# Early loads into the places of late weights, deeper places for exponents, POOL in the normalising, weights decoded in one width

## The chip, the cores and the metric

The kernel runs on one core of one Trainium2 chip. The metric is the device time of one execution in microseconds. One profiled execution, on which the rows below are read, took 704.23 us.

## The reference

Attention with four sink positions and a window of 128, over 4 batches, 8 heads, 768 positions and 64 columns a head, in float32; then a two-layer network on 3072 tokens of 512 columns, with 2048 hidden columns. Everything is checked at float32 accuracy; the weights arrive as float64.

```python
scores = scale * np.matmul(q, k.transpose(0, 1, 3, 2))
keep = is_sink | in_window
scores = np.where(keep, scores, -1000000000.0)
a = np.exp(scores - np.max(scores, axis=-1, keepdims=True))
a = a / (np.sum(a, axis=-1, keepdims=True) + 1e-09)
attn = np.matmul(a, v).astype(np.float32)
x = attn.transpose(0, 2, 1, 3).reshape(B * S, H * D)
h = x @ w_in
g = h - np.tanh(h)
out = (g @ w_out).astype(np.float32)
```

## The kernel before

**Tiling.** The 3072 tokens are 12 chunks of 256 (`chunks`, 3 in a batch). The first three chunks are the first chunks of batches 0 to 2. The attention of a chunk is four units, one for each pair of heads; unit `u` is pair `u % 4` of chunk `u // 4`. The network has 8 weight groups (`NG`), each with 256 hidden columns: `w_in` of a group is `(0, g)` and `w_out` is `(1, g)`. One step of the network is one chunk with one group, so there are 96 steps: 24 matmuls of the first half (L661, output `h`) and 12 of the second half (L709, output `o`). A product in float32 accuracy is made of a high part and a low part: `xh`, `xl`, `gh`, `gl`, and for weights two halves of a tile `w`.

**One unit.** `load_qk` loads keys and queries. `scores` multiplies them for two blocks of 128 queries, t = 0 and t = 1 (L457, or L450 for the first 12 units, which are called raw and use float32 as it is). `merge` (DVE: L468 and two of L474) applies the masks and takes the largest score; `exponent` (ACT, L482) exponentiates. `normalise` sums on DVE (L502, L503), scales on ACT (four of L508), and copies the sink columns on POOL (`sinks`, L513 to L515, tile `z`). `turn` transposes on PE (L532, tile `t`) and copies into the place `pts[:, m]`: once on ACT (`whole`, L539) and twice on DVE with masks (`part`, L546, below and after). `attend` closes a pair of units in the first three chunks: a transpose of `z` on PE (L563), copies of it on ACT (`zr`, L570), the product with the sink values (L580) and 16 matmuls with the values (L586), then `xh` on ACT (L598) and `xl` on DVE (L602). I call the 16 of L586 "the values".

**Weights.** `load_w` loads a group in two halves, `z` = 0 and 1, into tiles that are later overwritten by the decoded weights. `weights` turns each half of 512 numbers from float64 words into float32 with three operations on DVE (`_decode_part`, L154, L156, L158, tile `wm`), makes the high part on ACT (L634) and the low part on DVE (L640). All 16 tiles `(k, g)` have places of their own and stay to the end.

**Places.** Exponents `p` have two places (pool `pp`), chosen by `u % 2`. The copies of the transposes have four (`m = u % 4`). Raw queries have two tiles, so that the load of unit u waits for unit u - 2. Zeros around the queries of raw units are written by POOL for units 2 and 3 alone (L103), since later ones write on the same spots.

**Order.** The order of instructions on each engine is planned by `Work.order`: each piece of work has an engine, an assumed duration, a due time, and what it reads and writes. The planner runs through them and takes, on an engine that is free, the ready piece that is due first. `WAKE` is the assumed time from one engine's end to another's start, and `SLACK` comes on top where the waiting engine is PE. Engines then work strictly in that order, SP (which issues the loads) too. Steps of the network are ordered as `order` says: groups 0 and 1 for the first three chunks, then groups 2 to 7 for chunks 2 and 1, then chunk 0, then chunk after chunk.

**Ends.** The sums of the second half are kept in PSUM: `bank` says where (one tile `o` with two halves for most chunks). `collect` copies a half on ACT (L719) and `store` writes it out.

Of the kernel before, what the change touches and what calls it, by code (L numbers as in the profile page):

```python
# [9 lines left out]
F32 = mybir.dt.float32  # L10
# [156 lines left out]
class Work:  # L167
# [4 lines left out]
    WAKE = 80  # L172
    SLACK = 250
# [17 lines left out]
    def order(self):  # L191
# [15 lines left out]
        while any(waiting.values()):  # L207
# [9 lines left out]
            for u in users[n]:  # L217
                f = self.all[u][0]
                lag = 0 if f == e else self.WAKE + (self.SLACK if f == "PE" else 0)
# [7 lines left out]
def _banded(tc, qd, kp, vp, vs, masks, w_in, w_out, ident, pts, early, out):  # L227
    nc = tc.nc
    et = mybir.EngineType
    with ExitStack() as ctx:  # L230
# [6 lines left out]
        pp, sm = pool("pp", 2), pool("sm", 2)  # L237
# [6 lines left out]
        RAW, TWO, CUT, SPLIT, DUO = 12, 12, 2, 0, 3  # L244
# [8 lines left out]
        FIRST, EARLY, PACE, LEAD = 55000.0, 5000.0, 7200.0, 16000.0  # L253
        UNIT, SECOND, WLEAD, WNEXT = 3400.0, 0.0, 9000.0, 3500.0
# [22 lines left out]

        def unit(u):
            cc, p = divmod(u, NPAIR)
            return (cc, p, *chunks[cc])  # L280

        def slots(u):
            return [("kt", u if u < 2 else u % 2 + 2), ("qt", u if u < 2 else u % 2 + 2)]

        def load_qk(u):
            cc, p, b, c = unit(u)

            def keys():
# [12 lines left out]
            t = due_unit(u) - 8000
            work.add("SP", 500, t, keys, (), [slots(u)[0], "seq k"], lands=800)
# [27 lines left out]
        def load_w(k, g):  # L330
            def words():
                for z in range(2):
                    t = wraw[k, g, z] = wpool.tile([P, WG], I32, tag=f"w{k}_{g}_{z}", name=f"wraw{k}_{g}_{z}")
                    nc.sync.dma_start(t, (w_in, w_out)[k][g].bitcast(I32)[:, z * WG : (z + 1) * WG])

            t = due_group(g) + 3000 * k - 24000
            work.add("SP", 1000, t, words, (), [("wr", k, g)], lands=4100)
# [100 lines left out]
        def scores(u, t):  # L438
# [55 lines left out]
            work.add("DVE", 880 if kind else 450, d + 1000, merge, s + ["mask"] * (0 < kind), [("p", u % 2, i) for i in range(t, 2)])  # L494
            work.add("ACT", 780, d + 2000, exponent, (), [("p", u % 2, t)])

        def normalise(u):
# [11 lines left out]

            def sinks():  # L510
# [7 lines left out]
            ps = [("p", u % 2, 0), ("p", u % 2, 1)]  # L518
# [493 lines left out]
```

## Time and profile before

| | |
|---|---|
| median of three runs | 704.1 us (703.26 to 705.12) |
| the profiled execution | 704.23 us |
| its span in the trace | 702.5 us |
| PE busy in the span | 683.6 us (97%) |
| DVE busy | 437.4 us (62%) |
| ACT busy | 371.4 us (53%) |
| POOL busy | 49.3 us (7%) |

A busy PE is not a PE at its peak: its matmuls are pipelined and their ends are modelled. The page divides the span into slices and gives for each the busy share of an engine and the clock that PE was granted, as a share of the full one. The windows give the same for stretches that one chooses. Idle time is put down to the engine and the line that ended it, in square brackets in the timeline, behind a bar in the groups.

### The profile page before, as it was taken

What the parts mean: (1) busy time and instruction counts of PE and PEld (TensorE: products, weight loads), DVE (VectorE), ACT (ScalarE), POOL (GpSimd) and SP (SyncE); (2) the same over time, 40 slices, a digit from 0 to 9 for tenths busy, and PEclk for the clock granted to TensorE, in tenths of its full rate; (3) what the DMA queues carried; (4) which work ended last, traced back from release to release, by engine and by line L of the source; (5) the groups of instructions that cost most, each with busy time, mean ns of one, the idle gap of its engine ahead of it and who ended that gap; (6) DMA issues with size and microseconds to landing.
All of it is one profiled execution on the core that took longest, in us unless ns stands there. A gap on an engine that the chain in (4) does not pass through costs nothing.

```text
span 702.5 us, 12478 instructions
## 1 busy us (share of the span) xinstructions
PE 683.6 (97%) x4604; PEld 603.1 (86%) x4604; DVE 437.4 (62%) x1148; ACT 371.4 (53%) x1017; POOL 49.3 (7%) x186
## 2 busy tenths in 40 slices
PE   6979999999999999999999999999999999999996
PEld 4657889999989989988988998898898988998985
DVE  6898999984866456645665664664654755664121
ACT  5977443345756456545655555465555645644222
POOL 3221010000100000000001000001000000000000
PEclk9989999999999999999999999999999999999999
DMA  5877900002212012112103112111112101100001
GB/s 177 285 254 277 389 9 1 5 25 72 72 57 84 27 50 85 53 27 87 53 28 106 28 54 76 39 46 70 53 28 87 54 27 54 60 1 2 31 1 35
DMA packets 31713, 52.14 MB, mean 74 GB/s; under 512 B 3228, under 2 KB 21020, under 8 KB 31644
## 3 DMA queue, kind: packets, MB, share of 16 engines
q1 hardware_dynamic: 31644, 51.26, 22.5%
q8 instruction: 38, 0.62, 0.4%
q14 instruction: 31, 0.25, 0.1%
HBM read 44.96 MB, written 6.29 MB: 73 GB/s over the span
## 4 chain that ended last, share of the span: by engine, by line
PE 89%; DVE 4%; ACT 3%; DMA 1%; issue 1%; POOL 1%; SPq 0%; DVEq 0%; POOLq 0%; ACTq 0%
PE o L709 38%; PE h L661 37%; PE x L586 5%; PE s L457 5%; PE t L532 2%; PE s L450 1%; ACT p L508 1%; ACT p L482 1%; DMA wraw<-w_out 1%; PE x L580 1%; DVE p L474 1%; PE x L563 0%; ACT ob L719 0%; ACT zr L570 0%; DVE s L468 0%
## 5 line engine op out<-in xcount | busy, mean ns | idle before, releaser
L661 PE MATMUL h<-xh,w 128*128 128x256 f32 x1536 | 291.8, 281 | 0.6 <-DVE w L640 0.4
L661 PEld LDWEIGHTS h<-xh,w 128*128 128x128 f32 x1536 | 242.1, 188 | 2.5 <-DVE w L640 1.0
L661 PE MATMUL h<-xl,w 128*128 128x256 f32 x768 | 214.8, 280 | 1.7 <-DVE xl L602 1.7
L709 PE MATMUL o<-w,gh 128*128 128x512 f32 x768 | 198.2, 398 | 0.1
L709 PEld LDWEIGHTS o<-w,gh 128*128 128x128 f32 x768 | 137.4, 188 | 28.1 <-ACT gh L673 1.1
L661 PEld LDWEIGHTS h<-xl,w 128*128 128x128 f32 x768 | 144.4, 188 | 3.8 <-DVE xl L602 2.2
L709 PE MATMUL o<-w,gl 128*128 128x512 f32 x384 | 106.7, 398 | 0.7 <-ACT ob L719 0.7
L482 ACT ACTIVATE p<-p,st 128x132 f32<-128x132 f32 x192 | 76.0, 397 | 56.3 <-DVE st L474 55.7
L666 ACT ACTIVATE graw<-h 128x512 f32<-128x512 f32 x96 | 57.1, 595 | 91.3 <-PE h L661 91.2
L669 DVE TENSOR_TENSOR h<-h,graw 128x512 f32<-128x512 f32 x96 | 66.9, 696 | 54.1 <-ACT graw L666 53.3
L677 DVE TENSOR_TENSOR gl<-h,gh 128x512 fp32r<-128x512 f32 x96 | 66.2, 690 | 44.8 <-ACT gh L673 44.0
L709 PEld LDWEIGHTS o<-w,gl 128*128 128x128 f32 x384 | 70.9, 188 | 18.3 <-ACT ob L719 1.1
L468 DVE COPY_PREDICATED s<-above,s 128x256 f32<-128x256 uint32 x80 | 34.2, 427 | 80.7 <-PE s L457 79.4
L673 ACT CAST gh<-h 128x512 fp32r<-128x512 f32 x96 | 55.9, 582 | 43.5 <-DVE h L669 43.2
L508 ACT ACTIVATE p<-p,st 128x132 f32<-128x132 f32 x192 | 61.9, 395 | 5.0 <-DVE st L503 4.7
L474 DVE CUSTOM_DVE_ANT_0 p<-s,mask 128x132 f32<-128x132 f32 x192 | 49.0, 292 | 12.2 <-PE s L457 3.8
L513 POOL CAST z<-p 128x16 fp32r<-128x16 f32 x48 | 11.4, 237 | 524.2 <-ACT p L508 524.2
L457 PE MATMUL s<-ks,q 128*128 128x260 f32 x288 | 46.9, 285 | 0.2 <-DVE st L474 0.2
L457 PEld LDWEIGHTS s<-ks,q 128*128 128x128 f32 x288 | 42.4, 188 | 5.2 <-issue 0.7
L424 ACT CAST q<-qraw 128x512 fp32r<-128x512 f32 x36 | 22.3, 620 | 39.8 <-PE s L457 37.9
L586 PE MATMUL x<-pt,v 128*64 128x128 f32 (+1 forms) x512 | 43.0, 323 | 0.0
L586 PEld LDWEIGHTS x<-pt,v 128*64 128x64 f32 x512 | 31.7, 140 | 13.0 <-issue 6.4
(79 smaller groups left out, 571.5 us busy)
## 6 DMA issues: line engine op xcount, KB each, us to landing
qraw<-qd SPq DMA_DIRECT2D x36, 256.0 KB, 2.8
kraw<-kp SPq DMA_DIRECT2D x46, 196.0 KB, 2.7
wraw<-w_in SPq DMA_DIRECT2D x16, 512.0 KB, 6.5
wraw<-w_out SPq DMA_DIRECT2D x16, 512.0 KB, 8.7
v<-vp SPq DMA_DIRECT2D x27, 256.0 KB, 3.1
out<-ob SPq DMA_DIRECT2D x24, 256.0 KB, 2.0
qraw<-qd SPq DMA_DIRECT2D x20, 64.0 KB, 4.4
vraw<-vs SPq DMA_DIRECT2D x7, 64.0 KB
```

The lines of the kernel that those rows point to most:

```text
L457: nc.tensor.matmul(ps[h][:, :WIN], lhsT=q[:, h, t * P : (t + 1) * P], rhs=rhs, start=i == 0, stop=i == 1,)
L468: nc.vector.copy_predicated(both[:, :, TS:WIN], above.bitcast(U32).unsqueeze(1).to_broadcast([P, 2, P]), both[:, :, :P],)
L474: nc.vector.tensor_tensor_reduce(out=pr[u][:, j, :], in0=ps[h][:, P:WIN], in1=mask[:, kind, :], scale=-0.125, scalar=BIG, op0=ALU.add, op1 ...
L482: nc.scalar.activation(e, e, AF.Exp, bias=st[u][:, j : j + 1], scale=-1.0, accum_out=st[u][:, 4 + j : 5 + j],)
L508: nc.scalar.activation(pr[u][:, j, :], pr[u][:, j, :], AF.Copy, scale=s[:, 8 + j : 9 + j])
L586: nc.tensor.matmul(xps[key][(p - p0) // 2][h * 64 : h * 64 + 64, p % 2, a:z], lhsT=vt[cc, i][:, hd : hd + D], rhs=rhs, start=False, stop=p ...
L661: nc.tensor.matmul(hps[n][:, f, :], lhsT=w, rhs=x, start=r == 0, stop=r == 11)
L666: nc.scalar.activation(gr[n], hps[n], AF.Tanh)
L669: nc.vector.tensor_tensor(hps[n], hps[n], gr[n], op=ALU.subtract)
L673: nc.scalar.copy(gh[n], hps[n])
L677: nc.vector.tensor_tensor(gl[n], hps[n], gh[n].bitcast(F32), op=ALU.subtract)
L709: nc.tensor.matmul(ops[cc, t], lhsT=(gh, gh, gl)[i][n][:, f, t * P : (t + 1) * P], rhs=wt[1, g, f][:, (0, 1, 0)[i], 0, :], start=first and ...
```

## The change

- **Early loads.** Keys and queries of units 4 to 11 lie in places of the last weight groups: units 4 and 5 in that of `(1, 7)`, 6 and 7 in `(0, 7)`, 8 and 9 in `(1, 6)`, 10 and 11 in `(0, 6)` (`lent`). They are planned at the start, wait for no earlier unit, and the four weight loads come after them. POOL writes zeros over the whole query tile of each of units 2 to 11 (`zeros`, 128x512 each).
- **Exponents** of units 0 to 11 have four places (`slot`, `PB`), two of them in the pool `wmpool`, and their sums four tiles.
- **Normalising.** For units 3, 7 and 11 POOL multiplies the four blocks in one operation (`scale_all`) where ACT did it in four.
- **Wide decoding.** A group `(k, g)` is decoded as one tile of 1024 numbers, in `pts[:, 2]` or `pts[:, 3]`. Units 0 to 11 therefore have two places for the copies of the transposes (`place`), `u % 2`. The load is still two transfers.
- **The planner** has a `WAKE` for each engine, other assumed durations and due times. `sink_half` now comes before the first `merge`.
- **The last chunk** sums in two separate PSUM tiles, `t` and `x`.

```diff
-    WAKE = 80
-    SLACK = 250
+    WAKE = {"PE": 250, "ACT": 170, "DVE": 90, "POOL": 100, "SP": 80}
+    SLACK = 100
...
-        pp, sm = pool("pp", 2), pool("sm", 2)
+        pp, sm = pool("pp", 2), pool("sm", 4)
...
-        RAW, TWO, CUT, SPLIT, DUO = 12, 12, 2, 0, 3
+        RAW, TWO, CUT, DUO, SC, PB, ZL, TK = 12, 12, 2, 3, 4, 4, -4000, 1100
...
-        FIRST, EARLY, PACE, LEAD = 55000.0, 5000.0, 7200.0, 16000.0
-        UNIT, SECOND, WLEAD, WNEXT = 3400.0, 0.0, 9000.0, 3500.0
+        FIRST, EARLY, PACE, LEAD = 45000.0, 4600.0, 7200.0, 16000.0
+        UNIT, SECOND, WLEAD, WNEXT = 2000.0, 3000.0, 6000.0, 2500.0
...
+        def slot(u):
+
+            return u % PB if u < RAW else u % 2
...
+        lent = {u: (1 - (u - 4) // 2 % 2, NG - 1 - (u - 4) // 4) for u in range(4, RAW)}
...
+            def zeros():
+                if u in lent:
+                    qt[u] = lend()[:, : 2 * CH].rearrange("p (h s) -> p h s", h=2)
+                else:
+                    qt[u] = qpool.tile([P, 2, CH], F32, tag="qraw", name=f"qraw{u}")
+                nc.gpsimd.memset(qt[u], 0.0)
+
             t = due_unit(u) - 8000
+            if raw(u):
+                work.add("POOL", 460, t - ZL, zeros, (), [slots(u)[1]])
...
-                    pr[u] = pp.tile([P, 4, TS], F32, tag="p", name=f"p{u}")
+                    where, tag = (wmpool, "wm") if slot(u) > 1 else (pp, "p")
+                    pr[u] = where.tile([P, 4, TS], F32, tag=tag, name=f"p{u}")
...
+            def scale_all():
+                f = st[u][:, 8:12].unsqueeze(2).to_broadcast([P, 4, TS])
+                nc.gpsimd.tensor_tensor(pr[u], pr[u], f, op=ALU.mult)
...
-            work.add("ACT", 1200, d + 500, scale, [("st", u % 2)], ps)
+            if raw(u) and u % SC == SC - 1:
+                work.add("POOL", 1340, d + 500, scale_all, [("st", u % 4)], ps, port=True)
+            else:
+                work.add("ACT", 1200, d + 500, scale, [("st", u % 4)], ps)
...
+        def place(u):
+            return u % 2 if u < DUO * NPAIR else u % NPAIR
...
-        def weights(k, g, z):
-            key = (k, g, z)
-            slot = ("wm", count[0] % 2)
+        def weights(k, g):
+            key, r = (k, g), count[0] % 2
             count[0] += 1
+
+            wm[key] = pts[:, 2 + r].rearrange("p h a b -> p (h a b)")
...
-                work.add("DVE", (418, 692, 692)[i], d, lambda i=i: bits(i), [("wr", k, g)],
-                         [slot] + ["seq wm"] * (i == 0), port=True)
-            work.add("ACT", 530, d + 1000, high, [slot], [("w", *key)])
+                work.add("DVE", (684, 1224, 1224)[i], d, lambda i=i: bits(i), [("wr", k, g, 0), ("wr", k, g, 1)], [("dw", r)], port=True)
+            work.add("ACT", 985, d + 1000, high, [("dw", r)], [("w", *key)])
+            work.add("DVE", 1224, d + 1500, low, [("dw", r)], [("w", *key)], port=True)
...
-            return {1: f"s{t}", 2: "tx"[t]}.get(cc, f"o{t}")
+            return {1: f"s{t}", 2: "tx"[t], NCHUNK - 1: "tx"[t]}.get(cc, f"o{t}")
...
-            if cc == 2 and t == 0:
+            if cc in (2, NCHUNK - 1) and t == 0:
                 return ps_t.tile([P, 2, 2, P], F32, tag="t", name=f"o{n}_0").rearrange("p a b c -> p (a b c)")
...
-        for u in (2, 3):
+        for u in range(2, RAW):
             load_qk(u)
```

Three places show how the order moves. Names are `tile<-tiles read`, a number behind an underscore tells one buffer from another, and the lines are those of the kernel concerned.

DVE, around the masks of unit 11 (in before `t_1003`, in the change `t_935`); `wraw` are loaded weights, `wm` and `pt` what is being decoded, `w` the decoded weights. Before:

```order
L158 SCALAR_TENSOR_TENSOR wm_1_0_921<-wraw_1_0_539,wm_1_0_921 128x512
L677 TENSOR_TENSOR gl_983<-h_706,gh_968 128x512
L602 TENSOR_TENSOR xl_977<-x_0_911,xh_976 128x512
L154 TENSOR_SCALAR wm_1_1_1001<-wraw_1_1_541 128x512
L156 SCALAR_TENSOR_TENSOR wm_1_1_1001<-wraw_1_1_541,wm_1_1_1001 128x512
L546 TENSOR_TENSOR pt<-t_1003,below 128x2x128
L546 TENSOR_TENSOR pt<-t_1003,after 128x2x128
L158 SCALAR_TENSOR_TENSOR wm_1_1_1001<-wraw_1_1_541,wm_1_1_1001 128x512
L640 TENSOR_TENSOR w_1_0_994<-wm_1_0_921,w_1_0_994 128x512
L640 TENSOR_TENSOR w_1_1_1037<-wm_1_1_1001,w_1_1_1037 128x512
```

And in the change:

```order
L680 TENSOR_TENSOR w_0_834<-pt,w_0_834 128x1024
L707 TENSOR_TENSOR h_712<-h_712,graw_865 128x512
L154 TENSOR_SCALAR pt<-wraw_1_516 128x1024
L588 TENSOR_TENSOR pt<-t_884,below 128x2x128
L588 TENSOR_TENSOR pt<-t_884,after 128x2x128
L644 TENSOR_TENSOR xl_915<-x_0_854,xh_914 128x512
L715 TENSOR_TENSOR gl_933<-h_712,gh_901 128x512
L707 TENSOR_TENSOR h_843<-h_843,graw_925 128x512
L588 TENSOR_TENSOR pt<-t_935,below 128x2x128
L588 TENSOR_TENSOR pt<-t_935,after 128x2x128
L156 SCALAR_TENSOR_TENSOR pt<-wraw_1_516,pt 128x1024
```

In before `(1, 1)` is being decoded when unit 11's masks come; in the change only the first operation of `(0, 1)` stands ahead of them.

POOL, from the zeros of the last early queries to the first normalising. Before (units 3 to 1):

```order
L103 MEMSET qraw_313 64x256 x2
L513 CAST z<-p_275 128x2x8
L514 TENSOR_TENSOR z<-p_275,z 128x2x8
L515 CAST z<-z 128x2x16
L387 TENSOR_TENSOR vraw<-vraw,vsink 64x128 x2
L388 TENSOR_SCALAR vraw<-vraw,half 128x128
L513 CAST z<-p_300 128x2x8
L514 TENSOR_TENSOR z<-p_300,z 128x2x8
L515 CAST z<-z 128x2x16
L513 CAST z<-p_361 128x2x8
```

And in the change, where `qk` are the lent tiles and `p_387` is unit 3:

```order
L325 MEMSET qk_311 128x512 x2
L549 CAST z<-p_294 128x2x8
L550 TENSOR_TENSOR z<-p_294,z 128x2x8
L551 CAST z<-z 128x2x16
L418 TENSOR_TENSOR vraw<-vraw,vsink 64x128 x2
L419 TENSOR_SCALAR vraw<-vraw,half 128x128
L549 CAST z<-p_318 128x2x8
L550 TENSOR_TENSOR z<-p_318,z 128x2x8
L551 CAST z<-z 128x2x16
L544 TENSOR_TENSOR p_387<-p_387,st_388 128x528
L549 CAST z<-p_342 128x2x8
```

Ten zero fills of the whole tile now stand ahead of the first `z`, and a multiplication stands between two of them.

PE, its last products. Before:

```order
L709 MATMUL o_7365<-w_7_0_1848,gh_7641 128x512 x2
L709 MATMUL o_7365<-w_7_1_1879,gh_7641 128x512 x2
L709 MATMUL o_7365<-w_7_0_1848,gl_7645 128x512
L709 MATMUL o_7365<-w_7_1_1879,gl_7645 128x512
L709 MATMUL o_7365<-w_7_0_1848,gh_7641 128x512 x2
L709 MATMUL o_7365<-w_7_1_1879,gh_7641 128x512 x2
L709 MATMUL o_7365<-w_7_0_1848,gl_7645 128x512
L709 MATMUL o_7365<-w_7_1_1879,gl_7645 128x512
```

And in the change:

```order
L747 MATMUL o_1_7221<-w_6_1607,gl_7478 128x512 x2
L747 MATMUL o_0_7214<-w_7_1707,gh_7491 128x512 x4
L747 MATMUL o_0_7214<-w_7_1707,gl_7497 128x512 x2
L747 MATMUL o_1_7221<-w_7_1707,gh_7491 128x512 x4
L747 MATMUL o_1_7221<-w_7_1707,gl_7497 128x512 x2
```

The two halves are two tiles in the change, `o_0` and `o_1`; the order is the same.

## Rows read from the trace of the kernel before

**Rows 1.** The page, busy time, share and instructions of the matmul and weight-load engine

```profile
PE 683.6 (97%) x4604; PEld 603.1 (86%) x4604; DVE 437.4 (62%) x1148; ACT 371.4 (53%) x1017; POOL 49.3 (7%) x186
```

**Rows 2.** Windows: stretch, length, busy PE, PEld, DVE, ACT, POOL; clock, DMA share, GB/s

```profile
6.70:16.00 9.30, 6.09 (x25) 4.10 (x24) 6.59 (x40) 6.18 (x26) 2.12 (x7) 1.00 0.67 203
16.00:30.00 14.00, 13.63 (x79) 9.84 (x80) 12.39 (x55) 13.76 (x54) 3.12 (x11) 0.88 0.88 286
...
45.00:53.00 8.00, 5.49 (x25) 3.17 (x25) 6.68 (x21) 6.51 (x24) 3.36 (x9) 0.71 0.54 182
53.00:62.00 9.00, 8.03 (x43) 6.59 (x42) 6.48 (x30) 6.01 (x24) 1.29 (x4) 0.88 0.59 180
62.00:73.30 11.30, 11.03 (x79) 8.30 (x77) 10.71 (x30) 8.55 (x27) 1.91 (x6) 1.00 1.01 395
...
104.00:124.00 20.00, 20.00 (x130) 18.04 (x129) 18.55 (x32) 7.65 (x14) 0.00 (x0) 1.00 0.01 1
```

**Rows 3.** The same view, from DVE's first work in the main part to unit 11's masks

```profile
6.70:70.03 63.33, 54.07 (x300) 40.06 (x300) 53.99 (x214) 51.86 (x188) 16.34 (x46) 0.92 0.79 263
```

**Rows 4.** Timeline of DVE and PE, start and duration: unit 11's last mask, then what follows its values on PE

```profile
69.62 0.41 DVE L546 TENSOR_TENSOR pt<-t,after 128x256 f32<-128x256 f32 x1
...
73.26 1.20 PE L709 MATMUL o<-w,gh 128*128 128x512 f32 x4
```

**Rows 5.** Windows of lines 661 and 709 alone, busy PE, PEld; first L661

```profile
0.00:73.26 73.26, 9.35 (x54) 7.15 (x54) 0.93 0.76 255
...
0.00:73.26 73.26, 4.41 (x17) 2.79 (x17) 0.93 0.76 255
```

**Rows 6.** Groups from 6.7 to 70.03 us, DVE then ACT: busy us, mean ns | idle

```profile
L156 DVE SCALAR_TENSOR_TENSOR wm<-wraw,wm 128x512 uint32<-128x512 uint32 x8 | 5.5, 686 | 0.2
L546 DVE TENSOR_TENSOR pt<-t,below 128x256 f32<-128x256 f32 x12 | 5.1, 422 | 1.5 <-ACT pt L539 1.1 <-PE t L532 0.2
L640 DVE TENSOR_TENSOR w<-wm,w 128x512 fp32r<-128x512 f32 x6 | 4.2, 696 | 0.0
L154 DVE TENSOR_SCALAR wm<-wraw 128x512 uint32<-128x512 uint32 x8 | 3.4, 420 | 0.0
...
L365 DVE CAST half<-halfi 128x1 f32<-128x1 int32 x1 | 0.2, 154 | 0.0
...
L508 ACT ACTIVATE p<-p,st 128x132 f32<-128x132 f32 x48 | 15.5, 396 | 2.3 <-DVE st L503 2.3
L634 ACT CAST w<-wm 128x512 fp32r<-128x512 f32 x7 | 4.3, 616 | 0.5 <-DVE wm L158 0.5
```

**Rows 7.** Groups of POOL: from 6.7 to 73.3 us, then from 200 to 300 us

```profile
L514 POOL TENSOR_TENSOR z<-p,z 128x16 fp32r<-128x16 f32 x12 | 4.4, 364 | 1.0
L387 POOL TENSOR_TENSOR vraw<-vraw,vsink 64x128 f32<-64x128 f32 x6 | 2.7, 452 | 0.4 <-ACT vsink L383 0.2
...
L514 POOL TENSOR_TENSOR z<-p,z 128x16 fp32r<-128x16 f32 x7 | 1.5, 221 | 0.6
```

**Rows 8.** Timeline of DVE, then POOL, in the first three microseconds

```profile
2.14 0.23 DVE L119 CAST pt<-pt 128x128 f32<-128x128 int32 x1 [2.14 <-POOL pt L76]
2.33 0.41 DVE L120 CAST pt<-pt 128x128 f32<-128x128 int32 x1
...
2.36 0.70 POOL L103 MEMSET pt<- 64x256 f32 x2
```

**Rows 9.** Timeline: PE at two places, then DVE

```profile
22.68 1.92 PE L450 MATMUL s<-kraw,qraw 128*128 128x260 f32 x8
...
48.75 0.79 PE L580 MATMUL x<-zr,vsink 128*128 128x512 f32 x1 [1.74 <-ACT zr L570]
52.23 3.42 PE L450 MATMUL s<-kraw,qraw 128*128 128x260 f32 x8
...
54.48 0.29 DVE L474 CUSTOM_DVE_ANT_0 p<-s,mask 128x132 f32<-128x132 f32 x1 [2.63 <-PE s L450]
```

**Rows 10.** Timeline at the end of the program

```profile
696.57 0.73 PE L709 MATMUL o<-w,gl 128*128 128x512 f32 x2 [0.68 <-ACT ob L719]
```

More of the change, by code (lines that the diff above doesn't have):

```diff
@@ L493, in scores @@
             work.add("PE", took, d, products, src, s)
-            work.add("DVE", 880 if kind else 450, d + 1000, merge, s + ["mask"] * (0 < kind), [("p", u % 2, i) for i in range(t, 2)])
-            work.add("ACT", 780, d + 2000, exponent, (), [("p", u % 2, t)])
+            work.add("DVE", 880 if kind else 450, d + 1000, merge, s + ["mask"] * (0 < kind), [("p", slot(u), i) for i in range(t, 2)])
+            work.add("ACT", 780, d + 2000, exponent, (), [("p", slot(u), t)])
         def normalise(u):
@@ L548, in turn @@
             d = due_unit(u) + 5500
-            work.add("PE", 450, d, transposes, [("p", m % 2, 0), ("p", m % 2, 1)], ["t"])
+            work.add("PE", 470, d, transposes, [("p", slot(u), 0), ("p", slot(u), 1)], ["t"])
             if c == 0:
@@ L608, in attend @@
             v = [vslot[cc, i] for i in range(max(0, 2 * c - 1), 2 * c + 2)]
-            pt = [(f"pt {k}", m) for k in ("whole", "own", "before") for m in range(p0, p0 + pairs)]
+            pt = [(f"pt {k}", place(NPAIR * cc + i)) for k in ("whole", "own", "before") for i in range(p0, p0 + pairs)]
             need = pt + ["vsink", ("zr", 0), ("zr", 1)] + v
-            work.add("PE", 200 + 1100 * pairs, d + 3500, values, need, ["x", "t"][: pairs // 2])
+            work.add("PE", (340 + 735 * pairs if c == 0 else 200 + TK * pairs), d + 3500, values, need, ["x", "t"][: pairs // 2])
             for i in banks:
@@ L735, in first_half @@
                     x = [("xu", home(cc), 2 * z), ("xu", home(cc), 2 * z + 1), ("x", home(cc))]
[L736 removed]
+                    work.add("PE", 722, due_step(n), some, x + [("w", 0, g)], [("h", n % 2)])
         def second_half(n):
@@ L761, in _banded @@
         sink_values(0, 10000)
-        for g in range(NG):
-            for k in range(2):
+        mine = [(k, g) for g in range(NG) for k in range(2)]
+        for k, g in mine:
+            if (k, g) not in lent.values():
                 load_w(k, g)
-                for z in range(2):
-                    weights(k, g, z)
+                weights(k, g)
         def attention(cc):
@@ L788, in _banded @@
             attention(cc)
+        for k, g in mine:
+            if (k, g) in lent.values():
+                load_w(k, g)
+                weights(k, g)
         ends = [cc for cc, g in order if g == NG - 1]
```

76 lines of the change are left out of this document (42 added, 34 removed).

## Prediction

> **What bounds the kernel now.** I read the page first, then windows by stage, then the groups and the timeline of the early stage, last the end. PE is busy 683.6 of 702.5 us [rows 1], and from 73 us on it is simply full: 20.00 us of 20 in the window from 104 to 124 us [rows 2]. No instruction of PE is taken away, so the time can only fall by what PE loses before 73 us and at the very end. In the early stage PE lacks work or clock: the windows show 6.09 of 9.30, 5.49 of 8.00 and 8.03 of 9.00 us busy, and the granted clock is 0.88, 0.71 and 0.88 in three of them [rows 2]. That stage is the attention of the first three chunks. DVE and ACT carry it: from 6.70 to 70.03 us DVE is busy 53.99 and ACT 51.86 of 63.33 us [rows 3]. It ends with the masks of unit 11 (the last starts at 69.62 and ends at 70.03 us), and PE is through with that unit's values at 73.26 us [rows 4]. Whatever brings this point forward brings the end forward, as long as PE has done as much network work by then and is fed afterwards.
>
> By 73.26 us PE has begun 54 matmuls of the first half and 16 of the second (the row counts 17, the last begins at 73.26 itself) [rows 5]. In the new order 54 and 12 stand ahead of the same point. The new stage so carries 4 x 0.26 us (4.41 us for 17 [rows 5]) = 1.0 us less for PE, which has to be paid later.
>
> **Part 1: less decoding ahead of unit 11's masks.** This is the largest term. Ahead of them DVE now runs 8 of L154, 8 of L156, 7 of L158 (the eighth is the one cut by the window's edge; I take it at L156's duration) and 6 of L640: 8 x 0.420 + 15 x 0.686 + 6 x 0.696 = 17.8 us [rows 6]. In the new order there are 3 + 2 + 2 + 2 of the wide ones. The wide ones are not in the trace. Upper bound: twice the narrow ones, 0.84, 1.37 and 1.39 us, nothing won by width. Lower: the mask of 256 columns takes 0.422 and L640 of 512 takes 0.696 [rows 6], so 256 more columns cost 0.274 us and a fixed 0.15 us remains; then 0.69 for L154 and 1.24 for the others. I take the lower, since both of its forms are read in this stretch. New: 3 x 0.69 + 6 x 1.24 = 9.5 us (10.8 at the upper bound). One product gl less stands there, 0.7 us. DVE's work up to the masks falls by 17.8 - 9.5 + 0.7 = 9.0, from 54.0 to 45.0 us.
>
> **Part 2: ACT.** A scaling takes 15.5 us / 12 = 1.29 us [rows 6]; three of twelve go to POOL: -3.9. Seven casts of 0.616 us (4.3) become two wide ones, at 2 x 0.616 less the fixed 0.15 each: 2.2, so -2.1. One cast of gh less: -0.6. ACT falls from 51.9 to 45.3 us. But `sink_half`, eight small operations, now stands ahead of the first merge; the merge of unit 0 and ACT's first exponent slip by its length, 8 x 0.154 = 1.2 us [rows 6].
>
> **Part 3: POOL.** A multiplication of 128x528 is not in the trace. Between 128x16 at 0.221 us in quiet time and 64x128 at 0.452 [rows 7], 112 more columns cost 0.231 us: 0.22 + 512 x 0.0021 = 1.28 us, about what ACT needed, so a scaled unit gets its transposes no later, if POOL is free. Its risk is company: z copies of 0.221 us take 0.364 on average in the early stage [rows 7]. Beside wide decoding the delay can be one whole operation of 1.24 us instead of 0.69; over three scalings and twelve z copies I put this into the idle time.
>
> The zeros: ten fills of 512 columns where four halves stood. Two fills of 256 columns take 0.70 us [rows 8]; a wide one lies between 0.35 and 0.70, I take 0.55, so that POOL is done at about 11 us. POOL was idle then. But the first DVE work falls into these fills. A DVE cast that meets a fill takes 0.41 instead of 0.23 us [rows 8]. Eight fills are left when DVE begins: from 8 x 0.12 = 1.0 us, if each costs about half of what that cast lost and some, to 8 x 0.55 = 4.4 us, if each blocks DVE for its length. I take 1.0, nearest to the row. The Trainium skill, page "SBUF — State Buffer", section "SBUF: two separate sides", calls the port pair that VectorE and GpSimd share an exclusive lock, held for a whole instruction. The row of the cast agrees in kind, and by the rule alone the upper 4.4 us would be the price.
>
> **Part 4: loads and places.** SP no longer waits for a query tile before units 4 to 11. Loads stay in the same single order; PE is not kept by them except at units 4 and 5, and the DMA share is 0.9 there already [rows 2], so I book nothing. The value tiles still make SP wait for an earlier chunk's values with later loads behind them; those loads are units 9 to 11 and weights that are wanted several microseconds later. If that cover is gone it costs one landing, some 3 us. Four exponent places let scores and exponents run two units further ahead. Against it two places for the copies of the transposes mean that the masks of a pair wait for the values of the pair before, five times.
>
> **Idle time.** DVE has 63.33 - 53.99 = 9.3 us of idle time in the stretch [rows 3]. What goes: 2.63 us in one wait for scores behind slow matmuls [rows 9], and the waits of masks for ACT's copy, 1.1 us [rows 6]. What comes: the first merge behind the slipped start is inside DVE's own work, 1.0 us of port waits, and five hand-overs at 0.5 to 1 us. With 9.3 us again the masks end at 6.7 + 45.0 + 9.3 = 61.0 us. Taken by ACT, with its own idle time of 63.33 - 51.86 = 11.5 us [rows 3], its late start included, and the slip of 1.2 us, they would end at 6.7 + 45.3 + 11.5 + 1.2 = 64.7. I take 62.2 us, nearer to DVE's. From the last mask to the end of the values it is 73.26 - 70.03 = 3.2 us [rows 4], so 65.4 us where 73.26 stood: 7.9 us earlier, less the 1.0 us of network work: 6.9 us.
>
> **Part 5: after the stage.** PE is full if DVE delivers weights. Two steps need two weight tiles. For DVE now: 8 halves of operations, 4 x (0.420 + 2 x 0.686 + 0.696) = 9.95 us, and 4 x 0.69 for the network's own products, together 12.7 us; new: 2 x (0.69 + 3 x 1.24) + 2.8 = 11.6 us. PE needs 2 x 36 matmuls, and at 130 in 20 us [rows 2] that is 11.1 us. DVE operations overlap a little, so this is balanced, where before it lived on a lead. The lead in the new order is one tile at the end of the stage. I book nothing; at the upper bound of the wide price (12.7 us) six groups could lose up to 6 x 1.6 - 5 of lead = 4.6 us.
>
> **Part 6: the end.** The last two matmuls wait 0.68 us for ACT's copy of the other half of the same tile [rows 10]. In two tiles they don't: -0.7 us.
>
> Sum against the profiled execution: 704.23 - 6.9 - 0.7 = 696.6 us. That execution lies 0.1 us above the median of 704.1, so nothing is corrected. The planner's new waits also shift the order later on. Little can be won there, since half of the 18.9 us in which PE was idle in all [rows 1] lies in the early stretch [rows 3] and most of the rest ahead of it and at the end; I allow 1 us either way.
>
> **Rivals.**
> A, the forecast: 694 to 700 us.
> B, the deep places work better: idle time falls to half. ACT's work then sets the end, 6.7 + 45.3 + 11.5/2 + 1.2 = 59.0 us for the masks, 62.2 for the values: 11.1 - 1.0 + 0.7 earlier, 693 us, and 690 if three quarters go. For it: ACT and DVE wait mostly for each other. Against: DVE and ACT have 45 us of work each and PE 50 (12 units at 3.3 us, see C, and 66 network matmuls at 20/130 us), and three such engines in some 55 us leave no room.
> C, the clock. PE has no network work until unit 10 now, and the granted clock fell to 0.71 around the 1.74 us pause at 47 us; then eight matmuls of scores took 3.42 instead of 1.92 us [rows 2, 9]. PE was busy 54.07 us in the stretch [rows 3]; 70 network matmuls at 20/130 us [rows 2] are 10.8 of it, so a unit takes 43.3/12 = 3.6 us at a mean clock of 0.92, 3.3 at the full 2.4 GHz and 6.6 at 1.2 GHz, against 55.5/12 = 4.6 us a unit that the forecast leaves (62.2 - 6.7). Now about 10 us of the stage lie at 1.2 GHz (twice the missing share of the three windows' clocks: 3.4 + 4.6 + 2.2), and the forecast keeps them. With 32 us there, the other 22 cost 22 x (1 - 4.6/6.6) = 6.7 us: 703 us, no change.
> D, slower: the hand-over of two places. Where the masks of a pair come up on DVE before the values of the last pair are done, everything behind them in DVE's queue stands, merges too, and with them ACT and PE. The stretch from 47 to 55 us shows the price of such a chain (z, its copy, values, scores): 2.63 us on DVE, 1.74 on PE [rows 9]. One such stall at each of five hand-overs, 2.6 + 1.7 = 4.3 us, gives 21 us less the one there is now: 704.2 + 21 - 4.3 - 0.7 - 6.9 = 713 us at worst; from three stalls on (696.6 + 3 x 4.3 = 709) it is slower than before, with two it is even. Against it: four exponent places give DVE two units of merges to do meanwhile.
> E, the fills block at full length: 4.4 instead of 1.0 us, 700 us.
> F, starved after the stage: 696.6 + 2 to 4.6, 700 us.
> That wide decoding saves nothing is inside E and F: +1.3 us.
>
> **How the numbers follow.** A 0.54, B 0.12, C 0.14, D 0.09, E 0.08, F 0.03. A change of less than 0.3% (2.1 us) can't be told from none with this kernel. Faster than 702.0: A, B, E, F and a third of C, 0.81. Same: most of the rest of C, 0.09. Slower: D and a little of C, 0.10. The range of 8 in 10 leaves out D, half of C and what lies past three quarters of the idle time in B: 690 to 703 us.
>
> **What would show it.** In the profile of the changed kernel the masks of unit 11 end near 62 us and its values near 65 us, with 54 and 12 network matmuls ahead; DVE has some 45 us of work up to there and 9 to 10 idle; wide operations take 1.24 us; POOL's multiplication 1.3 us; PE has no gaps from 66 to 690 us and none before its last two matmuls. The prediction is wrong if the clock stays at 1.2 GHz for more than 30 us before 65 us, if DVE stands at masks behind values for 2 us and more, several times, or if gaps behind L680 (the low part of weights) appear on PE after 66 us.

## The result, and the profile after

The changed kernel takes 700.08 us in the median of four runs (699.38 to 700.25) against 704.1: a ratio of 0.9945, 95% interval 0.9927 to 0.9963. It is faster by 4.0 us; 7.5 were forecast. The profiled execution took 699.38 us, span 697.6.

The page's busy line of after, which answers [rows 1]:

```profile
span 697.6 us, 12381 instructions
...
PE 681.9 (98%) x4604; PEld 602.6 (86%) x4604; DVE 427.7 (61%) x1084; ACT 363.4 (52%) x989; POOL 55.5 (8%) x195
```

The windows of after over the stretches of [rows 2], and the one up to the last mask of unit 11, which answers [rows 3] (busy time of each engine, granted clock of PE, DMA share, GB/s):

```profile
6.70:16.00 9.30, 5.40 (x14) 3.77 (x14) 7.04 (x28) 2.68 (x13) 3.37 (x8) 0.82 0.72 227
16.00:30.00 14.00, 12.84 (x70) 9.00 (x69) 12.06 (x56) 13.43 (x56) 6.19 (x16) 1.00 0.59 185
45.00:53.00 8.00, 8.00 (x58) 6.63 (x58) 7.40 (x30) 7.91 (x32) 2.62 (x7) 1.00 0.72 245
53.00:62.00 9.00, 9.00 (x73) 7.87 (x71) 8.11 (x20) 6.00 (x15) 4.38 (x10) 1.00 0.98 343
104.00:124.00 20.00, 20.00 (x136) 18.27 (x135) 19.48 (x24) 6.24 (x9) 0.00 (x0) 1.00 0.01 4
...
6.70:63.46 56.76, 50.25 (x300) 38.39 (x300) 49.03 (x193) 45.63 (x173) 22.39 (x56) 0.97 0.78 253
```

The first stretch is worse than before [rows 2]: PE busy 5.40 us against 6.09, ACT 2.68 against 6.18, the clock 0.82 against 1.00. From 45 us on PE is full, where before it had 5.49 of 8.00 and 8.03 of 9.00. ACT's work is what was forecast (45.63; 45.3), DVE's is not (49.03; 45.0); some 3.0 of its 49.03 us are the waiting of three operations at the start, which the rows below show.

The end of the early stage in the timeline of after, which answers [rows 4], with the first operations of DVE and PE's first pause (start, duration, engine, line; the idle time ahead in brackets):

```profile
6.32 3.75 POOL L325 MEMSET qk<- 128x512 f32 x8
6.75 3.40 DVE L135 COPY mask<-mask 128x128 f32<-128x128 f32 x1 [1.90 <-issue]
6.89 3.27 DVE L136 COPY mask<-pt 128x4 f32<-128x4 f32 x1
6.96 3.26 DVE L137 TENSOR_SCALAR pt<-pt,lim 128x128 f32<-128x128 f32 x1
10.26 0.29 DVE L138 TENSOR_TENSOR pt<-pt 128x128 f32<-128x128 f32 x1
...
11.92 0.28 DVE L506 CUSTOM_DVE_ANT_0 p<-s,mask 128x132 f32<-128x132 f32 x1
...
12.64 3.43 PE L481 MATMUL s<-pt 128*128 128x260 f32 x8 [3.90 <-DMA qraw<-qd]
...
63.05 0.41 DVE L588 TENSOR_TENSOR pt<-t,after 128x256 f32<-128x256 f32 x1
...
63.96 0.40 PE L622 MATMUL x<-zr,vsink 128*128 128x512 f32 x1
...
65.73 0.73 PE L747 MATMUL o<-w,gh 128*128 128x512 f32 x2
```

The same places in before, its first merge and unit 11's product with the sink values:

```profile
6.71 0.29 DVE L135 COPY mask<-mask 128x128 f32<-128x128 f32 x1 [1.88 <-issue]
...
7.71 0.29 DVE L474 CUSTOM_DVE_ANT_0 p<-s,mask 128x132 f32<-128x132 f32 x1
...
71.48 0.40 PE L580 MATMUL x<-zr,vsink 128*128 128x512 f32 x1
```

Unit 11's masks end at 63.46 us and its values at 65.73: 62.2 and 65.4 were forecast, 70.03 and 73.26 stood before. As forecast, 54 and 12 network matmuls stand ahead. But the start is not the one forecast. POOL's eight fills run from 6.32 to 10.07 us, and three small DVE operations that started at 6.75 to 6.96 all end near 10.2. The first merge begins at 11.92 us, not at 8.9 (7.71 and the 1.2 of `sink_half`). What followed must have been faster than forecast. Below, "unit 11's values begin" means its product with the sink values, 63.96 us here and 71.48 before.

From the values' end to PE's last matmul (691.09 + 0.63) after needs 625.99 us. Before needed 624.04 (73.26 to 696.57 + 0.73); with four more matmuls of `o` (0.94) and without the last wait (0.68) it should be 624.3. So 1.7 us are lost where PE's rows show no gap. From PE's last matmul to the end of the span it is another 5.88 us, against 5.20.

### The profile page after: what moved, and what is told of

It is laid out like the page before. It is cut to its first block, busy times and chain, and to the rows that moved or that the text cites. A ratio compares the mean times of both kernels' runs of the same rounds, so it can differ in the third digit from the quotient of the medians.

```text
span 697.6 us, 12381 instructions
## 1 busy us (share of the span) xinstructions
PE 681.9 (98%) x4604; PEld 602.6 (86%) x4604; DVE 427.7 (61%) x1084; ACT 363.4 (52%) x989; POOL 55.5 (8%) x195
## 4 chain that ended last, share of the span: by engine, by line
PE 95%; DVE 1%; ACT 1%; POOL 1%; DMA 0%; issue 0%; POOLq 0%; DVEq 0%; ACTq 0%
PE o L747 39%; PE h L699 39%; PE x L628 6%; PE s L488 5%; PE t L574 3%; PE s L481 2%; PE x L622 1%; POOL qk L325 1%; ACT p L540 0%; DMA qraw<-qd 0%; PE x L605 0%; DVE pt L588 0%; DVE p L506 0%; ACT p L514 0%; ACT zr L612 0%
## 5 line engine op out<-in xcount | busy, mean ns | idle before, releaser
L514 ACT ACTIVATE p<-p,st 128x132 f32<-128x132 f32 x192 | 76.0, 399 | 53.9 <-DVE st L506 52.4
L540 ACT ACTIVATE p<-p,st 128x132 f32<-128x132 f32 x180 | 58.2, 395 | 10.1 <-DVE st L535 9.6
L588 DVE TENSOR_TENSOR pt<-t,below 128x512 f32<-128x512 f32 (+1 forms) x48 | 28.7, 597 | 38.5 <-PE t L574 36.6
L450 DVE TENSOR_TENSOR ks<-kraw,ks 64x392 fp32r<-64x392 f32 x72 | 40.4, 561 | 2.3
L628 PE MATMUL x<-pt,v 128*64 128x128 f32 (+1 forms) x512 | 41.5, 316 | 0.0
```

The costliest lines, as they stand in the source:

```text
L450: nc.vector.tensor_tensor(k[o, h, :], t[r, :], k[r, h, :].bitcast(F32), op=ALU.subtract)
L514: nc.scalar.activation(e, e, AF.Exp, bias=st[u][:, j : j + 1], scale=-1.0, accum_out=st[u][:, 4 + j : 5 + j],)
L540: nc.scalar.activation(pr[u][:, j, :], pr[u][:, j, :], AF.Copy, scale=s[:, 8 + j : 9 + j])
L628: nc.tensor.matmul(xps[key][(p - p0) // 2][h * 64 : h * 64 + 64, p % 2, a:z], lhsT=vt[cc, i][:, hd : hd + D], rhs=rhs, start=False, stop=p ...
```

## The experiments

Below, a ratio is always to before; after has 0.9945. No edit leaves work out.

The end of the stage is read from one execution each, and these differ. After and experiments 1, 4 and 5 have the same order up to there, yet unit 11's values begin at 63.96, 64.81, 64.27 and 65.74 us, with a granted clock of 0.82, 0.70, 0.68 and 0.77 from 6.7 to 16 us. A difference of 1 or 2 us between two such readings shows nothing by itself.

**1. The fills, first try.** The planner was told that the fills of the lent places come after the masks.

```diff
-                work.add("POOL", 460, t - ZL, zeros, (), [slots(u)[1]])
+                work.add("POOL", 460, t - ZL, zeros, ["mask", "half"] if u in lent else (), [slots(u)[1]])
```

> After, with one edit: POOL's eight zero fills of the lent places wait until DVE is through with its masks and sink_half. In after these fills ran as one block from 6.32 to 10.07 us and DVE's casts beside them took 3.3 to 3.4 us each; the first merge came at 11.92 us where it had stood at 7.71. Theory (the block is what it cost, and the stage passes it on): the first merge starts near 8.6 us, PE's pause of 3.90 us shrinks below 1 us, the values of unit 11 end 3 us earlier (near 62.7 us), and the time falls by 2.5 to 3.5 us against after, to about 697 us. Rival (the later fills only move the block: they meet DVE's masks of the first units and hold the loads of units 4 to 7 back): DVE work beside the fills from 9 to 14 us takes 1 us and more per operation, and the time stays within 1 us of after. Second rival (the start is set by the loads of units 2 and 3, which the pause of PE names): the first merge is early, but the values of unit 11 end within 1 us of 65.7.

Ratio 0.9951 (0.9932 to 0.9970): no change, and no test. The planner's names are not semaphores, and POOL still had nothing ahead of the fills, so they ran at 6.35 us, as in after, and L135 took 3.21 us.

**2. The fills moved.** Four run on ACT, which is idle then, and four on POOL behind unit 0's sinks. For that the loads of units 8 to 11 are planned later too, behind unit 0's normalising.

```diff
-                nc.gpsimd.memset(qt[u], 0.0)
+                if 4 <= u < 8:
+                    nc.scalar.activation(..., ident.unsqueeze(1).to_broadcast([P, 4, P]), AF.Copy, scale=0.0)
+                else:
+                    nc.gpsimd.memset(qt[u], 0.0)
...
+                e, took = ("ACT", 580) if 4 <= u < 8 else ("POOL", 460)
+                work.add(e, took, t - ZL, zeros, [("z", 0)] if u > 7 else (), [slots(u)[1]])
...
-        for u in range(2, RAW):
+        for u in range(2, 8):
             load_qk(u)
...
+                if u == 0:
+                    for i in range(8, RAW):
+                        load_qk(i)
```

> After, with the eight zero fills of the lent places taken from the start of POOL: four (units 4 to 7) run on ACT before its first exponent, where ACT is idle, and four (units 8 to 11) on POOL behind the copies of unit 0's sinks. PE's order is the same as in after. Theory (the run of eight fills held DVE's first operations for 3.3 us, and the stage passes that on): L135 to L137 take 0.3 us each, the first merge starts near 8.6 us instead of 11.92, PE's pause of 3.90 us falls below 1.5 us, unit 11's values end 2.5 to 3.5 us earlier, and the time falls by as much against after, to 697 us or a little below. Rival (the start is set by the loads of units 2 and 3 or by the lower granted clock): first merge early, but values of unit 11 within 1 us of after's 65.7, time within 1 us of after.

Ratio 0.9882 (0.9866 to 0.9899), 695.27 us: 4.4 us less than after. The timeline of its start (its lines lie 5 behind those of after from there on):

```profile
5.05 2.19 ACT L326 ACTIVATE qk<-ident 128x512 f32<-128x512 f32 x4
...
6.75 0.23 DVE L135 COPY mask<-mask 128x128 f32<-128x128 f32 x1 [1.91 <-issue]
6.89 0.16 DVE L136 COPY mask<-pt 128x4 f32<-128x4 f32 x1
6.97 0.28 DVE L137 TENSOR_SCALAR pt<-pt,lim 128x128 f32<-128x128 f32 x1
...
8.94 0.28 DVE L511 CUSTOM_DVE_ANT_0 p<-s,mask 128x132 f32<-128x132 f32 x1
...
9.66 1.99 PE L486 MATMUL s<-pt 128*128 128x260 f32 x8 [1.73 <-issue]
```

L135 takes 0.23 instead of 3.40 us, the first merge comes 3.0 us earlier, and PE pauses for 1.73 instead of 3.90 us. The 2.5 to 3.5 us expected at the stage's end don't show in the profile: unit 11's values begin at 62.61 us, 1.35 earlier than in after. That execution was the longest of the four (697.5; the others 694.8 to 695.7), with a granted clock of 0.88 from 16 to 30 us. Experiment 11 has the same order up to there and a clock of 1.00, and its values begin at 59.90. Since loads moved too, it is experiment 3 that shows the fills alone.

**3. The fills added to before.** Eight fills of the same size, behind those of units 2 and 3, into a place nobody uses yet; all else as in before.

```diff
+                    spare = pts[:, 3].rearrange("p h a b -> p h (a b)")
+                    for i in range(8 * (u == 3)):
+                        nc.gpsimd.memset(spare[:, i % 2], 0.0)
```

> Before, with eight added zero fills of 128x512 on POOL behind the fills of units 2 and 3, into the place of the fourth pair's transposes, which nothing uses at that time. Order and work of all other engines as in before. Theory (a run of fills holds DVE's first operations for its whole length): L119-like work is untouched, but the operations that start near 6.7 us take up to 3.4 us instead of 0.2 to 0.3, the first merge slips from 7.7 to about 11 us, and the time rises by 2 to 4.5 us against before. Rival (before's stage has slack at its start, with DVE waiting later anyway): first merge late, time within 1 us of before.

Ratio 1.007 (1.0051 to 1.0089), 708.9 us: 5 us slower, a little over the theory's range. The timeline, and two windows:

```profile
6.72 3.93 DVE L135 COPY mask<-mask 128x128 f32<-128x128 f32 x1 [1.88 <-issue]
6.83 3.75 POOL L300 MEMSET pt<- 128x512 f32 x8
...
11.23 0.29 DVE L477 CUSTOM_DVE_ANT_0 p<-s,mask 128x132 f32<-128x132 f32 x1
```

```profile
6.70:16.00 9.30, 5.53 (x14) 3.39 (x14) 7.64 (x28) 3.17 (x15) 3.87 (x9) 0.81 0.72 218
16.00:30.00 14.00, 12.04 (x56) 9.09 (x54) 9.07 (x41) 10.89 (x41) 3.37 (x12) 0.76 0.45 150
```

The first merge slips by 3.5 us, from 7.71 to 11.23. The rest of the 5 us fits the clock, though no run shows it apart: PE pauses for 3.2 us behind the late merges, and the clock of the first stretch falls to 0.81 and of the next to 0.76, where before has 1.00 and 0.88 [rows 2].

**4. Lags.** The planner's old lags for all work from the fourth chunk on; the early stage keeps its order.

```diff
+                lag = self.WAKE[e] + (self.SLACK if f == "PE" else 0) if u < self.late else 80 + (250 if f == "PE" else 0)
...
```

> After, with the planner's old lags (80 ns for every engine, 250 more towards PE) for all work from the fourth chunk on; the early stage keeps its order. This gives PE the old pattern of a later chunk (transposes between two pieces of the first half) in place of the new one (transposes directly ahead of second-half matmuls, twice a chunk). In after a later chunk takes 55.7 to 55.8 us from values to values, in before 55.4. Theory (in the new pattern the second-half matmuls stand at gh's cast, which ACT runs behind a scaling; 0.3 us twice a chunk, hidden in the trace under the transposes' modelled end): chunks take 55.4 us again, and the time falls by 1.5 to 2.5 us against after, to about 698 us. Rival (the loss after 66 us lies at the chunk's ends or in the decoding stretch up to 160 us): chunk times stay at 55.7, and the time within 0.5 us of after.

Ratio 0.9897 (0.9881 to 0.9913), 696.30 us: 3.4 to 3.8 us less than after, more than expected. One later chunk, first in after, then here:

```profile
374.37 1.30 ACT L540 ACTIVATE p<-p,st 128x132 f32<-128x132 f32 x4 [0.31 <-DVE st L535]
...
375.57 0.56 ACT L711 CAST gh<-h 128x512 fp32r<-128x512 f32 x1
375.61 0.60 PE L574 MATMUL t<-ident,p 128*128 128x128 f32 x4
...
376.19 0.30 PEld L747 LDWEIGHTS o<-w,gh 128*128 128x128 f32 x2 [0.22 <-ACT gh L711]
```

```profile
386.37 0.57 ACT L712 CAST gh<-h 128x512 fp32r<-128x512 f32 x1
386.56 0.60 PE L575 MATMUL t<-ident,p 128*128 128x128 f32 x4
...
387.70 0.63 PE L748 MATMUL o<-w,gh 128*128 128x512 f32 x2
```

In after the second half follows the transposes at once, and its weight load stands 0.22 us at ACT's cast of `gh`, which ends at 376.13 behind a scaling. Here six matmuls of the first half lie between, and `o` begins 0.76 us after the cast. From one chunk's product with the sink values to the next it is mostly 55.7 to 55.8 us in after and 55.4 here, as in before; eight such intervals take 444.4, 442.1 and 442.3 us. From the values' end to PE's last matmul it is 623.03 us here (66.05 to 689.08), 3.0 less than in after. All waits of this kind from 66 us on, in after, here and in before (in total, times, longest):

```profile
PEld o L747 <- ACT gh L711: 3.0, 14, 0.2
```

```profile
PEld o L748 <- ACT gh L712: 1.3, 5, 0.3
```

```profile
PEld o L709 <- ACT gh L673: 1.1, 5, 0.2
```

So the waits that the trace shows make up some 1.7 of the 3.0 us, and most of what after lost against before; the rest of the 3.0 is open. The rows of PE alone show no gap: the modelled 0.60 us of the transposes reaches over the wait.

**5. The end.** The last chunk's sums back in one tile (`bank` and `sums_of` without `NCHUNK - 1`).

> After, with the last chunk's two outputs back in the two halves of one PSUM tile. Theory (term of 0.7 us at the end): the last two matmuls wait some 0.7 us for ACT's copy of the other half, as in before (0.68), and the time rises by 0.7 us against after. Rival (the end is set by the first store's landing, or the last copy and store are not shortened by it): PE's wait is back, but the time stays within 0.3 us of after.

Ratio 0.9958 (0.9943 to 0.9974), 700.82 us: 0.7 us more in the median, too little for the intervals. The wait is back:

```profile
693.64 0.74 PE L747 MATMUL o<-w,gl 128*128 128x512 f32 x2 [0.68 <-ACT ob L758]
```

**6 and 7. ACT.** `SC` = 99 lets ACT scale all twelve units, `SC` = 2 gives six to POOL.

> After, with ACT scaling all twelve early units (POOL none). ACT has 3 x 1.3 = 3.9 us more work in the stage. Theory (DVE and PE set the stage now, ACT has slack): the values of unit 11 end within 1 us of 65.7 and the time stays within 0.7 us of after. Rival (ACT carries the stage with DVE): the stage ends 2 to 4 us later and the time rises by as much. Third way (POOL's multiplication holds the port, 1.89 us for the last one and 0.3 us on wide operations beside it): without it the stage ends earlier, by up to 1 us.

> After, with POOL scaling six of the twelve early units instead of three: 3.9 us less on ACT, three more multiplications of about 1.1 us on POOL, which hold the shared port. Theory (ACT carries the stage; with ACT scaling all twelve the time rose by 4.3 us): the stage ends 2 to 4 us earlier and the time falls by as much against after, to about 697 us. Rival (ACT and DVE are close, and DVE or POOL's blocking takes over at once): less than 1 us against after. Third way (POOL waits for wide decoding, so that a scaled unit's transposes come late): slower than after by 1 us and more, with multiplications of 1.5 us and more.

With twelve on ACT the ratio is 1.0007 (0.9996 to 1.0017), 704.39 us: 4.3 more than after, and nothing is left of the gain. With six on POOL it is 0.9962 (0.9949 to 0.9974), 700.54 us: no gain either. The window from 53 to 62 us, of twelve on ACT and then of six on POOL:

```profile
53.00:62.00 9.00, 8.44 (x53) 7.13 (x51) 8.17 (x29) 8.66 (x31) 3.62 (x9) 1.00 0.90 318
```

```profile
53.00:62.00 9.00, 8.96 (x73) 7.56 (x72) 8.52 (x25) 7.14 (x22) 4.39 (x7) 1.00 0.95 324
```

ACT is full in the one (8.66 of 9.00). But that the 4.3 us are near the 3.9 us of work moved to ACT is luck, for most of the loss lies behind the stage. Unit 11's values begin 4.0 us later there (67.96), but with 54 and 22 network matmuls ahead instead of 54 and 12; ten of the second half are 2.35 us of work (at 0.94 for four), so the stage itself costs some 1.7 us. Then, from 74 to 78 and 78 to 84 us:

```profile
74.00:78.00 4.00, 1.65 (x13) 1.41 (x12) 3.97 (x5) 2.51 (x4) 0.00 (x0) 1.00 1.06 403
78.00:84.00 6.00, 6.00 (x28) 5.09 (x27) 5.96 (x8) 1.75 (x3) 0.00 (x0) 0.72 1.02 376
...
77.67 2.86 PE L747 MATMUL o<-w,gh 128*128 128x512 f32 x8 [2.35 <-ACT gh L711]
```

PE has done that work early, pauses for 2.35 us until `gh` of the next step is made, and is then granted a clock of 0.72; in after it is busy all of both stretches at 1.00. So the edit shows that the order with all scalings on ACT is worth nothing, not that ACT's work sets the end of the stage.

With six on POOL, ACT has 7.14 and DVE 8.52, and PE is as full as in after, so the time freed on ACT shortens nothing. The third way did not occur: POOL's six multiplications take 1.06 to 1.07 us each.

**8. Two places for exponents** (`PB` = 2).

> After, with two places for early exponents instead of four (units alternate between two). Everything else as in after, though the planner moves work around the shorter lead. Theory (four places let merges and exponents run ahead, and that removed most of the idle time of the early stage and its dip of the clock at 47 us): the stage ends 3 to 6 us later, with waits of merges for scaled or transposed places, and the time rises by as much against after. Rival (the gain came from moving and widening decoding, and depth adds nothing): within 1 us of after.

Ratio 1.0019 (1.0008 to 1.0029), 704.78 us: 4.7 more than after. Waits of DVE and ACT between 12 and 72 us (in total, times, longest):

```profile
DVE p L506 <- PE t L574: 2.2, 3, 0.9
...
ACT pt L581 <- PE t L574: 5.7, 6, 2.2
```

Merges wait for the place that an earlier unit's transposes still read, which doesn't occur in after, and ACT's wait for transposes is 5.7 us against 2.0 there. DVE's idle time up to the last mask (69.33 us) is 10.4 us instead of 7.7. Unit 11's values begin at 71.16 instead of 63.96 us; since eight more matmuls of the second half stand ahead (1.9 us), the stage costs some 5.3 us.

**9. Due times.** Before with after's due times alone, and after with those of before (`FIRST`, `EARLY`, `UNIT`, `SECOND`, `WLEAD`, `WNEXT`).

> Before, with only the planner's due times of after (FIRST, EARLY, UNIT, SECOND, WLEAD, WNEXT); lags, places, narrow decoding, ACT's scalings and loads as in before. Ahead of unit 11's masks DVE then runs 6, 6, 6 and 5 decoding halves instead of 8, 8, 7 and 6: 4.3 us less. Theory (DVE's work sets the end of the stage, the step that carries most of the predicted gain): unit 11's values end some 3 to 4 us earlier than 73.3, and the time falls by 2 to 4 us against before. Rival (ACT's work, or the chain of waits between ACT and DVE, sets it): within 1.5 us of before.

> After, with the due times of before (FIRST, EARLY, UNIT, SECOND, WLEAD, WNEXT). Ahead of unit 11's masks DVE still runs only 3, 3, 2 and 2 wide decoding operations, because the lent places and the planner's other lags hold the rest back; the order of the early stage changes in places, later chunks keep the order of after. Theory (due times act through the amount of decoding ahead of the stage's end alone): within 1.5 us of after. Rival (due times also set how scores, merges and network matmuls interleave): 2 us slower and more, with waits of PE or DVE in the stage.

The first has 0.9949 (0.9931 to 0.9966), 699.39 us: by itself as much as the whole change. Unit 11's values begin at 68.02 us, where before they began at 71.48: 3.5 us for 3.6 less decoding ahead (2 x 0.420 + 3 x 0.686 + 0.696 by [rows 6]; the 4.3 of the expectation was added up wrongly). The window up to its last mask:

```profile
6.70:66.81 60.11, 50.27 (x302) 38.08 (x302) 51.05 (x208) 50.73 (x188) 14.48 (x47) 0.97 0.83 275
```

Against [rows 3] DVE's work is 2.9 us less and its idle time nearly the same (9.1; 9.3). But due times move other work too, and the granted clock is 0.97 against 0.92, so that less decoding alone did it is not shown apart. The profiled execution took 701.51 us, 2.1 more than the median.

The second has 0.9955 (0.9942 to 0.9968), 700.46 us: in after's places the due times add nothing in time, though unit 11's values begin at 66.27 us in its profile. Nearly the same wide operations stand ahead either way (3, 3, 2 and 2 against 3, 2, 2 and 2).

**10. Width.** Every wide operation of decoding and of the low part as two of half the width, in the same place.

```diff
-                _decode_part(nc, wm[key].bitcast(U32), lo, hi, i)
+                for z in range(2):
+                    c = slice(z * DM, (z + 1) * DM)
+                    _decode_part(nc, wm[key].bitcast(U32)[:, c], lo[:, c], hi[:, c], i)
...
```

> After, with each wide decoding operation and each subtraction of the low part issued as two of half the width, in the same place of the order. Durations of before give 2 x (0.42 + 2 x 0.69 + 0.70) = 5.0 us a weight tile instead of 0.68 + 3 x 1.22 = 4.3 us: 0.65 us more per tile on DVE, two tiles in the early stage and about eleven in the stretch from 66 to 150 us, in which DVE is busy 19.3 to 19.5 of 20 us. Theory (DVE just keeps up with PE in that stretch, by the width alone): PE starves there, and the time rises by 3 to 7 us against after. Rival (DVE's operations overlap or a lead is left): the decoding stretch gets longer on DVE, PE stays full, and the time rises by less than 1.5 us, all of it from the early stage.

Ratio 0.9948 (0.9935 to 0.9961), 699.72 us: no change. Its window from 104 to 124 us:

```profile
104.00:124.00 20.00, 20.00 (x135) 18.22 (x135) 19.86 (x37) 6.41 (x10) 0.00 (x0) 1.00 0.01 4
```

And the group of one line on DVE from 66 to 160 us, here and then in after (busy, mean ns):

```profile
L158 DVE SCALAR_TENSOR_TENSOR pt<-wraw,pt 128x512 uint32<-128x512 uint32 x28 | 18.0, 682 | 0.0
```

```profile
L158 DVE SCALAR_TENSOR_TENSOR pt<-wraw,pt 128x1024 uint32<-128x1024 uint32 x14 | 17.2, 1232 | 0.3
```

DVE is busy 19.86 of 20 us, PE still all 20: the width is worth nothing that can be measured in the time. In the early stage DVE's work up to the last mask is 50.15 us, 1.1 more than in after, and yet the masks end at 63.66 us, 0.2 later, with the same granted clocks (0.82 from 6.7 to 16 us, then 1.00): there DVE's work alone does not set the end.

**11. Fills moved and old lags together.**

> After with two of the edits together: the eight fills moved off POOL's start (alone it took the ratio to before from 0.9945 to 0.988) and the old planner lags for work from the fourth chunk on (alone 0.990). Theory (the two losses lie in different stretches, the start and the later chunks, and add): ratio 0.982 to 0.985, about 692 us; chunks of 55.4 us, first merge near 8.9 us. Rival (the earlier start is taken back later, or the clock's dip after 16 us grows): ratio 0.987 and more.

Ratio 0.984 (0.9828 to 0.9853), 691.96 us: the two gains add (0.0063 and 0.0048 by themselves, 0.0105 together), and this version beats both kernels. Its first two windows have a full clock:

```profile
6.70:16.00 9.30, 7.49 (x33) 5.32 (x32) 7.43 (x45) 6.63 (x29) 2.44 (x7) 1.00 0.69 217
16.00:30.00 14.00, 11.89 (x79) 8.65 (x78) 13.08 (x57) 13.73 (x54) 6.21 (x16) 1.00 0.90 290
...
59.90 0.40 PE L628 MATMUL x<-zr,vsink 128*128 128x512 f32 x1
```

Unit 11's values begin at 59.90 us, 4.1 before those of after.

## Why the prediction was right or wrong

The sign, the place of the gain and the range held. The size did not: 696.6 was forecast for an execution that took 699.38. Of these 2.8 us, 0.3 lie in the early stage, 1.7 in the later chunks and 0.7 behind PE's last matmul. That the early stage comes so near is luck: its errors cancel, and profiles of one order differ there by more.

**Parts 1 and 2, the work.** The prices came out: 0.685 us for L154 (in quiet time; 0.69 taken) and 1.22 for the others (1.24), ACT's work to 0.3 us. That less decoding ahead of unit 11's masks brings the stage's end forward fits the due times alone, 3.5 us, but they move other work as well. The width, which the prediction counted as part of the saving, gave nothing: 1.1 us of DVE's work moved the masks by 0.2. So the step from DVE's work to the stage's end holds only in part. POOL's multiplication took 1.07 us twice and 1.89 once; 1.28 were forecast.

**Part 3, the port.** This is the first step that failed. The term was 1.0 us "nearest to the row" of one cast that met one fill; it measured 3.0 us (L138 begins at 10.26 us in after and at 7.28 in experiment 2). A row of one meeting did not tell what eight fills back to back do. Rival E had the mechanism, with 4.4 us of blocking; that its 700 us are the time measured is partly luck, since 1.7 us of the later chunks and 0.7 behind PE's last matmul are in it. The rule of the Trainium skill ("SBUF — State Buffer", section "SBUF: two separate sides") that I set aside was nearer: an exclusive lock. The trace adds one thing: DVE did not get in between two fills, all three waiting operations ended behind the last. In the time the fills cost 4.4 us (experiment 2) to 5 (experiment 3), more than their wait; behind them PE pauses for 3.90 us in after and 3.2 in experiment 3, and the granted clock falls to 0.82 and 0.81.

**Idle time.** Here an error the other way hid the one of Part 3. Up to the masks' end, taken at 62.2 us, the forecast left DVE 45.0 us of work, 1.0 of port waits and 9.5 of other idle time. Measured were 46.0 (49.03 less 3.0), 3.0 and 7.7 (56.76 - 49.03). So the first merge came 3.0 us late, the masks only 1.3. What was missed is the depth of four places, which Part 4 named and the sum priced at nothing (rival B alone had it): without it 4.7 us are gone and DVE stands idle 2.7 us longer (experiment 8). The masks' end was set nearer to DVE's estimate (61.0) than to ACT's (64.7); which of the two engines sets it no run shows apart.

**Part 4 and rivals C and D.** The hand-over of two places cost nothing that shows: DVE's masks wait for ACT's copy (2.7 us in all, five times, 0.9 at most), none for values. In the profile of after the clock was 1.00 from 16 us on; the dip at 47 us is gone.

**Part 5, after the stage.** Starving did not occur, as forecast, and at narrow width neither; with all scalings on ACT it did, for 2.35 us. What failed is the sentence that the planner's new lags shift the order later by 1 us either way: undoing them for the later chunks gave 3.4 us. Some 1.7 us of it is the wait of 0.2 us, twice in most chunks; where the rest comes from is open. I named gaps on PE as the sign, and these waits show only at its weight loads.

**Part 6, the end.** The wait of 0.68 us is gone and comes back with the old bank. In the profiled execution the time from PE's last matmul to the span's end was longer by as much. Experiment 11 has 5.1 us there with the same end (683.79 + 0.63 to 689.5), and experiments 4 and 10 have 5.05 and 5.24, so the 5.88 of after belong to that run, not to the change; why is open.

What each part is worth does not add up: due times alone give the whole 4 us, and without the four places or without POOL's scaling the whole 4 us are gone. Each of these edits also changes the planned order, so the order as a whole is what was tested. How much of the 11.6 us of experiment 11 (703.54 to 691.96) belongs to early loads alone wasn't tried, nor were the new lags in the early stage, the two places for the transposes and the earlier `sink_half`.

## What to carry to other kernels

Price contention by the length of the whole run of operations that holds a port, not by one meeting, and put fills on an engine that is idle and doesn't share the port. When an order is replanned for one stage, compare the pattern of the steady part as well: here a change of pattern that the busy shares don't show took back 3.4 us, nearly as much as the whole gain of 4.0. Undo each part alone before crediting it, and look where the loss lies: here the width gave nothing, a few due times gave as much as all the rest, and scalings moved back to ACT cost most of their time behind the stage, in a pause of PE.

## What the runs showed of the hardware

- Eight POOL fills of 128x512 took 3.75 us (0.47 each) and kept three DVE operations issued within 0.3 us from ending for 3.3 to 3.9 us. Whether each of them met the fills, or the second and third stood behind the first, the trace does not tell.
- POOL's multiplication of 128x528 took 1.07 us twice, beside merges of DVE, which kept their 0.30 us, and 1.89 once, issued 0.23 us behind a wide operation of DVE (L680). L154 and L680 issued behind the first two took 0.97 and 1.50 us instead of 0.685 and 1.22.
- ACT writes zeros of 128x512 by a scaled copy in 0.55 us each (four in 2.19) beside DVE, without slowing it.
